# The products of exp(k) with v: two head pairs behind each other in two slots, in place of four slots

## The chip, the core and the metric

One NeuronCore of a Trainium2 chip runs the whole program. The metric is device time in microseconds, the median of several executions. The profile shows one further execution, recorded instruction by instruction. Engines are named as the profile names them: PE (TensorE, matmuls), PEld (its weight loads), DVE (VectorE), ACT (ScalarE), POOL (GpSimd), SP (SyncE, which issues the loads and stores).

## The reference

Linear attention over 8 batches of 8 heads with 576 tokens and 64 channels, followed by a two-layer network on the 4608 tokens, all in float32:

```python
q_s = softmax over channels of q;  k_s = softmax over tokens of k
kv  = einsum('bhsd,bhse->bhde', k_s, v)      # 64 x 64 per head
att = einsum('bhsd,bhde->bhse', q_s, kv)     # tokens x 512 when heads are joined
h   = att @ w_in                             # 512 -> 2048
g   = max(h, 0) + log1p(exp(-abs(h)))
out = g @ w_out                              # 2048 -> 512
```

## The kernel before, in words

**Tiles and slots.** The 4608 tokens are cut into 9 tiles of 512. Tile t is one *stage* of the program (stage 0 to 8). The network's 2048 inner channels are cut into 16 blocks of 128; block j of tile t is one *slot* (slot 0 to 15 of stage t). In a slot TensorE first does `up(t, j)`: 12 matmuls of 128x512, a value split into a high and a low float32r part, three products for each of four head pairs, into one of two PSUM tiles `ph`. Then, two slots late, it does `down` for an earlier block: 12 matmuls into four PSUM tiles `po`. In stage 0 the split is not used, and there are eight float32 matmuls in a slot.

**Softplus.** Between `up` and `down`, ScalarE runs Abs, Exp, Copy and Ln (L384 to L387) and casts the result (`g_hi`, L395); VectorE runs three combined operations (L388 to L390) and the difference `g_lo` (L396). The cast and `g_lo` of a slot stand in the program of the next slot.

**Attention, spread over the slots.** While stage t runs, `attend(t + 1)` puts the attention of the next tile into its slots. A list `steps` of 17 entries names which step stands in which slot; `lazy` registers a unit's steps and their slots. For batch t + 1 there are four units `kv_unit`, one for each pair of heads, with six steps:

- `top`: maximum of k over tokens on VectorE (L182); the maximum over partitions follows, by a TensorE transpose in batches 1 and 2 (`ON_PE`), from batch 3 on by GpSimd (L187);
- `across`: only in batches 1 and 2: a second maximum and transpose (L198, L199);
- `shift`: subtraction of the maximum on VectorE (L203);
- `product`: Exp on ScalarE (L209); the matmuls of exp(k) with v (L214, ten in the program, each 64 columns wide, alternating between the upper and lower half of one of two PSUM tiles, `banks`, named att in the profile) are put behind the slot's `down`. Behind them `kv_prefetch` loads a later pair into the buffer that they free (`kp` has two buffers);
- `scale`: 1/sum, on VectorE (L224, L225);
- `split`: `kv_hi` on ScalarE (L238) and `kv_lo` on VectorE (L241).

The softmax of q (`q_unit`, 12 steps, L265 to L304) stands in slots 3 to 10. In slots 11 to 14, `x_unit` joins both, one head pair in each slot: a transpose on VectorE (L321) into the same PSUM tile, a cast on ScalarE (`q_hi`, L325), a difference on VectorE (`q_lo`, L326), and the matmuls L331 to L333 at the slot's end; the results are split in the next slot (L339, L340), those of the last two pairs behind slot 15.

In stages 0 and 1 there is also the preparation of weights (L115 to L146); the last of it, a split of 1.2 us on VectorE in each slot (L145, L146), runs through slot 14 of stage 1.

**Order.** All of this is written out by hand under `manual_schedule`: each engine runs its instructions in the order in which the program issues them. Within a slot it is `up`, the attention's steps (units in the order of registration: kv, then q, then x), `split_g` of the slot before, `softplus`, `down`, and last the matmuls kept back by `later`.

Of the kernel before, what the change touches and what calls it, by code (L numbers as in the profile page):

```python
# [54 lines left out]
def tile_attn_ffn(  # L55
# [38 lines left out]
    def load_w(k):  # L94
        raw[k] = wp.tile([P, 2, DM], I64, name=f"w{k}")
        nc.sync.dma_start(out=raw[k][:, 0], in_=w_in[k])
        nc.sync.dma_start(out=raw[k][:, 1], in_=w_out[k])
# [24 lines left out]
    def sign_w(k, engine=nc.vector):  # L122

        if engine is nc.vector:
            high, low = (raw[k].bitcast(U8).rearrange("p z (n e) -> p (z n) e", e=8)[:, :, e] for e in (7, 3))
            engine.tensor_scalar(out=low, in0=high, scalar1=0x80, scalar2=None, op0=ALU.bitwise_and)  # L126
        else:
            engine.tensor_scalar(
                out=halves(k, BF16)[1], in0=words(k, F32)[1], scalar1=2.0**-100, scalar2=2.0**-100,
                op0=ALU.mult, op1=ALU.mult,  # L130
            )
# [123 lines left out]
    def q_load(t):  # L255
        qt = qp.tile([P, HP * TOK], F32, name="qt")
        nc.sync.dma_start(out=qt, in_=q[:, HP * START[t]:HP * START[t + 1]])
        qtiles[t] = qt.rearrange("p (h n) -> p h n", h=HP)
# [58 lines left out]
    def x_unit(t, h, ps):  # L317


        def flip():  # L320
            nc.vector.transpose(ps, qtiles[t][:, h])  # L321

        def product():
            q_hi, q_lo = (qp.tile([P, TOK], F32R, name=name) for name in ("q_hi", "q_lo"))
            nc.scalar.copy(q_hi, ps)  # L325
            nc.vector.tensor_tensor(out=q_lo, in0=ps, in1=q_hi.bitcast(F32), op=ALU.subtract)  # L326

            def products():
                for b, c0, c1 in segments(t):
                    hi, lo = kv_hi[b % 2][h], kv_lo[b % 2][h]  # L330
                    nc.tensor.matmul(ps[:, c0:c1], lhsT=hi, rhs=q_hi[:, c0:c1], start=True, stop=False)  # L331
                    nc.tensor.matmul(ps[:, c0:c1], lhsT=lo, rhs=q_hi[:, c0:c1], start=False, stop=False)
                    nc.tensor.matmul(ps[:, c0:c1], lhsT=hi, rhs=q_lo[:, c0:c1], start=False, stop=True)  # L333

            later(products)

        def split():
            x = x_part(t, h)
            nc.scalar.copy(x[:, 0], ps)  # L339
            nc.vector.tensor_tensor(out=x[:, 1], in0=ps, in1=x[:, 0].bitcast(F32), op=ALU.subtract)  # L340

        return [flip, product, split]

    def x_first(h, bank):


        def flip():
            nc.vector.transpose(qT[:, h], qtiles[0][:, h])

        def product():  # L350
            nc.tensor.matmul(bank, lhsT=whole[:, h], rhs=qT[:, h], start=True, stop=True)

        def take():
            if h % 2 == 0:
                nc.scalar.copy(x0[:, h], bank)
            else:
                nc.vector.tensor_copy(x0[:, h], bank)

        return [flip, product, take]
# [75 lines left out]
    def kv_prefetch(**place):  # L435
        if ahead[0] < len(kv_order):
            bh = kv_order[ahead[0]]
            loaded[bh] = kv_load(*bh, **place)
            ahead[0] += 1

    with tc.manual_schedule():

        make_identity(nc, ident)
        q_load(0)
        for i in range(HP):
            place = dict(pool=xp, tag=f"x{i - 1}", shape=(P, HP * TOK)) if i >= 2 else {}
            kv_prefetch(engine=nc.vector, queue=nc.scalar, **place)
        for k in range(5):
            load_w(k)
        nc.vector.memset(zero, 0.0)  # L450

        nc.scalar.activation(ln1, zero, AF.Ln, bias=1.0)
        whole = wp.tile([P, HP, P], F32, name="spare")
        qT = wp.tile([P, HP, TOK], F32, name=f"w{NJ - 1}")
        x0 = xp.tile([P, HP, TOK], F32, name="x0")
        for z in [whole] + [z.bitcast(F32) for i in range(2) for z in kv_hi[i] + kv_lo[i]]:
            nc.vector.memset(z, 0.0)

        po = [ps_o.tile([P, DM], F32, name=f"po{h}") for h in range(HP)]
        units = [kv_unit(0, h, po[h]) for h in range(HP)]
        first = [x_first(h, po[h]) for h in range(HP)]
        todo = {f"q{i}": fn for i, fn in enumerate(q_unit(0))}
        for h in range(HP):
            todo.update({f"u{h}{i}": fn for i, fn in enumerate(units[h])})
            todo.update({f"x{h}{i}": fn for i, fn in enumerate(first[h])})
        for k in range(2):
            for name, fn in (("t", top_w), ("m", scale_w), ("s", lambda k: sign_w(k, nc.gpsimd)), ("j", join_w)):
                todo[f"{name}{k}"] = lambda k=k, fn=fn: fn(k)  # L470
        todo["kv"] = kv_prefetch
        todo["w"] = lambda: [load_w(k) for k in range(5, 10)]
        todo["q"] = lambda: [q_load(1)] + [load_w(k) for k in range(10, NJ)]
        for name in (
            "q0 q1 u00 q2 q3 q4 q5 u10 u01 u11 u02 u12 q6 u03 u13 u20 u30 u21 u31 u22 u32 u23 u33 t0 m0 s0 q7 q8 "
            "kv kv w u04 u14 u05 u15 q9 q10 q11 x00 x10 x01 x11 u24 u34 u25 u35 x20 x30 x02 x12 t1 m1 s1 x21 x31 j0 "
            "x22 x32 q"
        ).split():
            todo[name]()

        def attend(t):

            steps = [[] for _ in range(NJ + 1)]

            def lazy(make, slots):
                unit = []

                def step(i):
                    def fn():
                        if not i:  # L490
                            unit.extend(make())
                        unit[i]()
                    return fn

                for i, s in enumerate(slots):
                    steps[s].append(step(i))

            if t < B:
                on_pe = 1 if t <= ON_PE else 0
                for h in range(HP):  # L500
                    a = 2 * h
                    lazy(
                        lambda h=h: kv_unit(t, h, banks[h % 2], after=kv_prefetch),
                        [a, a + on_pe, a + 1 + on_pe, a + 2 + on_pe, a + 3 + on_pe, a + 3 + on_pe],
                    )
            lazy(lambda: q_unit(t), [3, 4, 5, 5, 6, 7, 8, 7, 8, 9, 9, 10])
            for h, slots in enumerate(([11, 11, 12], [12, 12, 13], [13, 13, NJ], [14, 14, NJ])):
                lazy(lambda h=h: x_unit(t, h, banks[h % 2]), slots)
            if t + 1 < NTILE:
                steps[14].append(lambda: q_load(t + 1))  # L510
            return steps

        order = [(t, j) for t in range(NTILE) for j in range(NJ)]
        pending, soft, waiting = [], None, []
        for n in range(len(order) + 3):
            slot = order[n] if n < len(order) else None
            if slot:
                t, j = slot
                if j == 0:
                    steps = attend(t + 1) if t + 1 < NTILE else [[] for _ in range(NJ + 1)]  # L520
                ph = up(t, j)
                for fn in steps[j]:
                    fn()
                if t == 0 and 1 <= j <= HP:
                    split_whole(j - 1)
                if t == 0 and j + 1 < NJ:
                    join_w(j + 1)
                for k in range(NJ):
                    if n == 10 + 4 * k // 3:
                        split_w(k)  # L530
                if j == NJ - 1:
                    for fn in steps[NJ]:
                        fn()
            if soft:
                pending.append((soft[0], split_g(soft[1]) if soft[0][0] else soft[1]))
                soft = None
            if slot:
                soft = slot, softplus(t, j, ph)
                if t == 0 and j + 2 < NJ:
                    for fn in (top_w, scale_w, sign_w):  # L540
                        fn(j + 2)
            while pending and order.index(pending[0][0]) <= n - 2:
                (t, j), g = pending.pop(0)
                down(t, j, g)
            for products in waiting:
                products()
            waiting.clear()
# [37 lines left out]
```

## Time and profile before

| | us |
|---|---|
| median of 3 runs (lowest, highest) | 929.53 (928.31, 929.96) |
| profiled execution | 928.47 |
| its span | 926.6 |
| PE busy | 886.7 (96%) |
| DVE busy | 703.8 (76%) |
| ACT busy | 581.7 (63%) |

The span runs from the first to the last instruction recorded; the execution's own time is 1.9 us longer. The mean granted clock of TensorE is 0.993 of full speed. A busy share is an average over stages with different limits. Stages begin at 34.55 (0), 160.63 (1), 267.24 (2), 361.69 (3), 456.02 (4), 550.83 (5), 645.43 (6), 740.25 (7) and 830.03 (8), by the first `up` matmul of each in the timeline of PE.

### The profile page before, as it was taken

How to read it: one execution, taken by the hardware profiler on the slowest of the kernel's cores; microseconds unless marked ns; L12 is line 12 of the kernel's file. 1: busy time of each engine (PE TensorE's matmuls, PEld its weight loads, DVE VectorE, ACT ScalarE, POOL GpSimd, SP SyncE). 2: the span in 40 equal slices, each digit the busy share in tenths (PEclk: the TensorE clock that was granted, in tenths of full speed). 3: DMA queues.
4: the chain of work that ended last, by engine and by line, in shares of the span. 5: the costliest groups of instructions: out<-in, count | busy, mean ns of one | idle time of the engine just before them, and what ended most of it. 6: DMA issues, size and time to landing. Idle time of an engine off the chain costs nothing.

```text
span 926.6 us, 11575 instructions
## 1 busy us (share of the span) xinstructions
PE 886.7 (96%) x4180; PEld 675.3 (73%) x4180; DVE 703.8 (76%) x1095; ACT 581.7 (63%) x982; POOL 56.4 (6%) x118
## 2 busy tenths in 40 slices
PE   2698999999899999999999999999999999999998
PEld 2243444677688888888888888888888888888886
DVE  8679888788878877787778778877787757765553
ACT  3666676756666656666567566656665666566554
POOL 1302200000001100110011000100110000000000
PEclk9899999999999999999999999999999999999999
DMA  9970101111013101210121012101200110001001
GB/s 315 381 298 26 35 17 46 45 53 52 1 46 97 52 1 46 89 43 18 46 71 52 27 46 71 52 26 46 71 27 1 46 46 1 1 1 46 0 1 46
DMA packets 49034, 55.28 MB, mean 60 GB/s; under 512 B 2256, under 2 KB 39120, under 8 KB 47824
## 3 DMA queue, kind: packets, MB, share of 16 engines
q1 hardware_dynamic: 48400, 54.27, 17.4%
q8 instruction: 33, 0.54, 0.2%
q10 hardware_dynamic: 576, 0.26, 0.1%
q14 instruction: 25, 0.20, 0.1%
HBM read 45.09 MB, written 9.44 MB: 59 GB/s over the span
## 4 chain that ended last, share of the span: by engine, by line
PE 76%; DVE 12%; ACT 8%; issue 3%; DMA 1%; POOL 0%; SPq 0%; DVEq 0%; ACTq 0%; POOLq 0%
PE ph L372 11%; PE ph L374 11%; PE ph L373 11%; PE po L418 11%; PE po L416 11%; PE po L417 11%; PE ph L367 3%; PE po L412 3%; PE att L214 2%; DVE w L126 1%; DVE l L390 1%; DVE w L389 1%; DVE w L388 1%; PE att L331 1%; ACT u L385 1%
## 5 line engine op out<-in xcount | busy, mean ns | idle before, releaser
L372 PE MATMUL ph<-x,w 128*128 128x512 f32 x480 | 191.7, 399 | 0.0
L418 PE MATMUL po<-w,g_lo 128*128 128x512 f32 x480 | 187.0, 390 | 1.4 <-DVE g_lo L396 1.4
L374 PE MATMUL ph<-x,w 128*128 128x512 f32 x480 | 188.0, 392 | 0.0
L373 PE MATMUL ph<-x,w 128*128 128x512 f32 x480 | 187.6, 391 | 0.0
L416 PE MATMUL po<-w,g_hi 128*128 128x512 f32 x480 | 186.8, 389 | 0.0
L417 PE MATMUL po<-w,g_hi 128*128 128x512 f32 x480 | 186.7, 389 | 0.0
L388 DVE SCALAR_TENSOR_TENSOR w<-w,u 128x512 f32<-128x512 f32 x128 | 88.4, 691 | 108.8 <-ACT w L386 108.8
L395 ACT CAST g_hi<-l 128x512 fp32r<-128x512 f32 x128 | 79.7, 622 | 92.3 <-DVE l L390 89.8
L390 DVE SCALAR_TENSOR_TENSOR l<-l,ln,w 128x512 f32<-128x512 f32 x128 | 96.3, 752 | 15.7 <-DVE w L389 1.4
L418 PEld LDWEIGHTS po<-w,g_lo 128*128 128x128 f32 x480 | 90.1, 188 | 21.2 <-DVE g_lo L396 2.6
L372 PEld LDWEIGHTS ph<-x,w 128*128 128x128 f32 x480 | 90.8, 189 | 19.3 <-issue 0.6
L374 PEld LDWEIGHTS ph<-x,w 128*128 128x128 f32 x480 | 90.4, 188 | 19.7
L417 PEld LDWEIGHTS po<-w,g_hi 128*128 128x128 f32 x480 | 90.1, 188 | 18.7
L416 PEld LDWEIGHTS po<-w,g_hi 128*128 128x128 f32 x480 | 90.1, 188 | 18.6
L373 PEld LDWEIGHTS ph<-x,w 128*128 128x128 f32 x480 | 90.7, 189 | 17.6 <-DVE w L146 0.2
L384 ACT ACTIVATE u<-ph 128x512 f32<-128x512 f32 x134 | 80.1, 598 | 33.5 <-PE ph L374 25.0
L396 DVE TENSOR_TENSOR g_lo<-l,g_hi 128x512 fp32r<-128x512 f32 x128 | 88.4, 691 | 15.5 <-ACT g_hi L395 15.3
L387 ACT ACTIVATE l<-u 128x512 f32<-128x512 f32 x128 | 79.3, 619 | 25.8 <-DVE g_lo L396 25.2
L389 DVE SCALAR_TENSOR_TENSOR w<-ph,w 128x512 f32<-128x512 f32 x128 | 88.5, 691 | 4.4
L385 ACT ACTIVATE u<-u 128x512 f32<-128x512 f32 x134 | 84.7, 632 | 4.3
L386 ACT ACTIVATE w<-u 128x512 f32<-128x512 f32 x128 | 80.9, 632 | 4.1
L325 ACT CAST q_hi<-att 128x512 fp32r<-128x512 f32 x32 | 18.8, 587 | 78.6 <-DVE att L321 78.6
(125 smaller groups left out, 1061.1 us busy)
## 6 DMA issues: line engine op xcount, KB each, us to landing
kvt<-in_kv SPq DMA_DIRECT2D x30, 512.0 KB, 4.2
qt<-in_q SPq DMA_DIRECT2D x9, 1024.0 KB, 4.9
w<-in_w_in SPq DMA_DIRECT2D x16, 512.0 KB, 10.2
w<-in_w_out SPq DMA_DIRECT2D x16, 512.0 KB, 10.2
out<-w SPq DMA_DIRECT2D x32, 256.0 KB, 2.3
kvt<-in_kv_tail SPq DMA_DIRECT2D x28, 64.0 KB, 3.9
x<-in_kv SPq DMA_DIRECT2D x2, 512.0 KB, 9.4
out<-x SPq DMA_DIRECT2D x4, 256.0 KB, 2.4
```

Of the source, the lines that this page charges most:

```text
L372: nc.tensor.matmul(ph, lhsT=w_hi, rhs=x_hi, start=h == 0, stop=False)
L373: nc.tensor.matmul(ph, lhsT=w_lo, rhs=x_hi, start=False, stop=False)
L374: nc.tensor.matmul(ph, lhsT=w_hi, rhs=x_lo, start=False, stop=h == HP - 1)
L385: nc.scalar.activation(u, u, AF.Exp, scale=-1.0)
L386: nc.scalar.activation(w, u, AF.Copy, bias=1.0)
L388: nc.vector.scalar_tensor_tensor(out=w, in0=w, scalar=1.0, in1=u, op0=ALU.subtract, op1=ALU.subtract)
L389: nc.vector.scalar_tensor_tensor(out=w, in0=ph, scalar=0.0, in1=w, op0=ALU.max, op1=ALU.subtract)
L390: nc.vector.scalar_tensor_tensor(out=l, in0=l, scalar=ln1, in1=w, op0=ALU.subtract, op1=ALU.add)
L396: nc.vector.tensor_tensor(out=g_lo, in0=l, in1=g_hi.bitcast(F32), op=ALU.subtract)
L416: nc.tensor.matmul(po, lhsT=g_hi[:, ms], rhs=w_hi, start=j == 0, stop=False)
L417: nc.tensor.matmul(po, lhsT=g_hi[:, ms], rhs=w_lo, start=False, stop=False)
L418: nc.tensor.matmul(po, lhsT=g_lo[:, ms], rhs=w_hi, start=False, stop=j == NJ - 1)
```

## The change

Only the slots of the steps of `kv_unit` are different, and only for t > 1, so in `attend(2)` to `attend(7)`, which run in stages 1 to 6. The first and second pair form a couple, and the third and fourth. Within a couple `top` and `shift` stand one slot apart, and `product`, `scale` and `split` stand in the same slots. No instruction is added or removed.

```diff
--- before.py
+++ after.py
@@ -499,9 +499,15 @@
                 on_pe = 1 if t <= ON_PE else 0
                 for h in range(HP):
                     a = 2 * h
+                    slots = [a, a + on_pe, a + 1 + on_pe, a + 2 + on_pe, a + 3 + on_pe, a + 3 + on_pe]
+                    if t > 1:
+
+                        a = (5 + on_pe) * (h // 2)
+                        c = a + h % 2 + on_pe
+                        slots = [c - on_pe, c, c + 1] + [a + on_pe + i for i in (3, 4, 4)]
                     lazy(
                         lambda h=h: kv_unit(t, h, banks[h % 2], after=kv_prefetch),
-                        [a, a + on_pe, a + 1 + on_pe, a + 2 + on_pe, a + 3 + on_pe, a + 3 + on_pe],
+                        slots,
                     )
             lazy(lambda: q_unit(t), [3, 4, 5, 5, 6, 7, 8, 7, 8, 9, 9, 10])
             for h, slots in enumerate(([11, 11, 12], [12, 12, 13], [13, 13, NJ], [14, 14, NJ])):
```

The slots that this gives (top, across, shift, product, scale, split; `across` does nothing from batch 3 on):

| pair | stage 1 before | stage 1 after | stages 2 to 6 before | stages 2 to 6 after |
|---|---|---|---|---|
| 0 | 0 1 2 3 4 4 | 0 1 2 4 5 5 | 0 0 1 2 3 3 | 0 0 1 3 4 4 |
| 1 | 2 3 4 5 6 6 | 1 2 3 4 5 5 | 2 2 3 4 5 5 | 1 1 2 3 4 4 |
| 2 | 4 5 6 7 8 8 | 6 7 8 10 11 11 | 4 4 5 6 7 7 | 5 5 6 8 9 9 |
| 3 | 6 7 8 9 10 10 | 7 8 9 10 11 11 | 6 6 7 8 9 9 | 6 6 7 8 9 9 |

On TensorE, at the end of a slot in stage 3, the program before has one pair's matmuls between the last `down` matmuls (po3) and the next slot's `up` (ph). This is slot 2:

```order
L417 MATMUL po3_2767<-spare_755,g_hi_2697 128x512
L418 MATMUL po3_2767<-spare_755,g_lo_2698 128x512
L214 MATMUL att0_105<-kvt_2182 64x65 x10
L372 MATMUL ph_2796<-x2_2452,w2_901 128x512
L373 MATMUL ph_2796<-x2_2452,w2_901 128x512
L374 MATMUL ph_2796<-x2_2452,w2_901 128x512
```

After the change, slot 2 has none, and at the end of slot 3 there are two, into both att tiles:

```order
L418 MATMUL po3_2767<-w0_786,g_lo_2751 128x512
L214 MATMUL att0_105<-kvt_2266 64x65 x10
L214 MATMUL att1_106<-kvt_2282 64x65 x10
L372 MATMUL ph_2856<-x2_2452,w3_929 128x512
L373 MATMUL ph_2856<-x2_2452,w3_929 128x512
L374 MATMUL ph_2856<-x2_2452,w3_929 128x512
```

So the matmuls of the second pair moved from the end of slot 4 to the end of slot 3, behind those of the first, which moved there from slot 2.

On VectorE, at the beginning of slot 9 of stage 3, between the last operation of softplus (L390) and that of the next slot, the program before has one pair's `scale` and `split` (L224 to L241, att1), then the last steps of q (L265 to L304), then `g_lo` (L396):

```order
L390 SCALAR_TENSOR_TENSOR l_3093<-l_3093,ln1_109,w_3092 128x512
L224 TENSOR_SCALAR r_3142<-att1_106 128x1
L225 RECIPROCAL r_3142<-r_3142 128x1
L241 SCALAR_TENSOR_TENSOR kv_lo03_100<-att1_106,r_3142,kv_hi03_92 64x64 x2
L265 COPY other_3149<-s_2818 32x64 x4
L300 SCALAR_TENSOR_TENSOR s_2818<-s_2818,other_3149 128x64
L301 RECIPROCAL s_2818<-s_2818 128x64
L304 TENSOR_TENSOR qt_2562<-qt_2562,s_2818 128x1024
L396 TENSOR_TENSOR g_lo_3158<-l_3093,g_hi_3157 128x512
```

After the change it has two pairs' in the same place:

```order
L390 SCALAR_TENSOR_TENSOR l_3070<-l_3070,ln1_109,w_3069 128x512
L224 TENSOR_SCALAR r_3135<-att0_105 128x1
L225 RECIPROCAL r_3135<-r_3135 128x1
L241 SCALAR_TENSOR_TENSOR kv_lo02_99<-att0_105,r_3135,kv_hi02_91 64x64 x2
L224 TENSOR_SCALAR r_3142<-att1_106 128x1
L225 RECIPROCAL r_3142<-r_3142 128x1
L241 SCALAR_TENSOR_TENSOR kv_lo03_100<-att1_106,r_3142,kv_hi03_92 64x64 x2
L265 COPY other_3149<-s_2796 32x64 x4
L300 SCALAR_TENSOR_TENSOR s_2796<-s_2796,other_3149 128x64
L301 RECIPROCAL s_2796<-s_2796 128x64
L304 TENSOR_TENSOR qt_2562<-qt_2562,s_2796 128x1024
L396 TENSOR_TENSOR g_lo_3158<-l_3070,g_hi_3157 128x512
```

The group that reads att0 moved here from slot 7; what follows it is in the same order as before.

## Rows read from the trace of the kernel before

**Rows 1.** The page: busy time, share of the span and instructions of each engine.
```profile
PE 886.7 (96%) x4180; PEld 675.3 (73%) x4180; DVE 703.8 (76%) x1095; ACT 581.7 (63%) x982; POOL 56.4 (6%) x118
```

**Rows 2.** Busy time by stage, stages 1 and 3 (columns: window, length, engines, clock, DMA).
```profile
160.63:267.24 106.61, 100.82 (x491) 77.63 (x490) 86.38 (x132) 70.55 (x116) 1.88 (x12) 0.98 0.13 43
...
361.69:456.02 94.33, 94.23 (x489) 77.06 (x488) 74.55 (x120) 60.21 (x107) 6.36 (x16) 1.00 0.15 48
```

**Rows 3.** Timeline of TensorE, stage 5, slots 2 and 3 (start, length, instruction).
```profile
566.70 0.39 PE L417 MATMUL po<-spare,g_hi 128*128 128x512 f32 x1
566.92 0.39 PE L418 MATMUL po<-spare,g_lo 128*128 128x512 f32 x1
567.24 0.80 PE L214 MATMUL att<-kvt 128*64 128x65 f32 x20
567.97 0.50 PE L372 MATMUL ph<-x,w 128*128 128x512 f32 x1
568.31 0.40 PE L373 MATMUL ph<-x,w 128*128 128x512 f32 x1
```

**Rows 4.** Groups of VectorE by line (busy, mean of one, idle before).
```profile
L182 DVE TENSOR_REDUCE mx<-kvt 128x128 f32<-128x640 f32 x30 | 39.8, 1328 | 1.8 <-DMA kvt<-in_kv_tail 1.3 <-DMA kvt<-in_kv 0.4
...
L296 DVE TENSOR_REDUCE s<-qt 128x32 f32<-128x1024 f32 x18 | 21.7, 1212 | 0.0
...
L203 DVE TENSOR_TENSOR kvt<-kvt,mx 128x640 f32<-128x640 f32 x20 | 16.5, 826 | 0.4
```

**Rows 5.** Timeline of ScalarE, stage 3, slot 8.
```profile
409.60 0.74 ACT L209 ACTIVATE kvt<-kvt 128x640 f32<-128x640 f32 x1
410.24 1.04 ACT L293 ACTIVATE qt<-qt 128x1024 f32<-128x1024 f32 x1
411.58 0.62 ACT L395 CAST g_hi<-l 128x512 fp32r<-128x512 f32 x1 [0.30 <-DVE l L390]
412.11 0.59 ACT L384 ACTIVATE u<-ph 128x512 f32<-128x512 f32 x1
```

**Rows 6.** Timeline of VectorE, stage 3, slot 9 and the start of 10.
```profile
416.25 0.15 DVE L224 TENSOR_SCALAR r<-att 128x1 f32<-128x1 f32 x1
...
417.96 0.78 DVE L265 COPY other<-s 32x64 f32<-32x64 f32 x4
...
419.04 0.55 DVE L301 RECIPROCAL s<-s 128x64 f32<-128x64 f32 x1
...
420.77 0.68 DVE L396 TENSOR_TENSOR g_lo<-l,g_hi 128x512 fp32r<-128x512 f32 x1
...
422.89 0.75 DVE L390 SCALAR_TENSOR_TENSOR l<-l,ln,w 128x512 f32<-128x512 f32 x1
423.56 1.22 DVE L304 TENSOR_TENSOR qt<-qt,s 128x1024 f32<-128x1024 f32 x1
```

**Rows 7.** Timeline of VectorE and TensorE, slot 13 of stages 3 and 6.
```profile
442.82 0.69 DVE L326 TENSOR_TENSOR q_lo<-att,q_hi 128x512 fp32r<-128x512 f32 x1 [0.65 <-ACT q_hi L325]
...
443.57 0.39 PE L331 MATMUL att<-q_hi,kv_hi 128*128 128x256 f32 x1
...
726.33 0.69 DVE L326 TENSOR_TENSOR q_lo<-att,q_hi 128x512 fp32r<-128x512 f32 x1 [0.65 <-ACT q_hi L325]
...
727.43 0.36 PE L331 MATMUL att<-q_hi,kv_hi 128*128 128x448 f32 x1
```

**Rows 8.** Waits of weight loads, stages 2 to 6 (total, times, longest).
```profile
PEld att L331 <- DVE q_lo L326: 2.9, 8, 0.5
```

**Rows 9.** Timeline of VectorE and TensorE, stage 1, slots 1, 4 and 11.
```profile
172.49 0.69 DVE L388 SCALAR_TENSOR_TENSOR w<-w,u 128x512 f32<-128x512 f32 x1 [2.75 <-ACT w L386]
...
190.62 1.32 DVE L182 TENSOR_REDUCE mx<-kvt 128x128 f32<-128x640 f32 x1 [1.33 <-DMA kvt<-in_kv_tail]
...
239.31 0.33 PE L331 MATMUL att<-q_hi,kv_hi 128*128 128x128 f32 x1 [1.76 <-DVE q_lo L326]
```

**Rows 10.** The page: DMA issues (times, KB each, us to landing).
```profile
kvt<-in_kv SPq DMA_DIRECT2D x30, 512.0 KB, 4.2
```

## The prediction, on record before the changed kernel ran

> **What bounds the kernel now.** I read the page first: TensorE is busy for 96% of the span [rows 1], so at first sight only TensorE's time counts. A table by stage (a stage is the 16 slots of one token tile) says the same for most of the run: stage 3 has 94.23 us of TensorE in 94.33, and stage 1 has only 100.82 in 106.61 [rows 2]. The timeline of TensorE gives its rates. Matmuls of 128x512 start every 0.227 us, so a slot of 24 costs 5.44 us. The products of one head pair (20 short matmuls in the trace) take 0.73 us, and around them two steps are longer than 0.227: 0.32 into them and 0.34 out of them [rows 3].
>
> "Busy" hides a second bound. In slots 11 to 14 TensorE needs, at the end of the slot, the `q_lo` that VectorE makes in that slot. In slot 13 of stage 3, `q_lo` ends at 442.82 + 0.69 = 443.51 and TensorE's L331 starts at 443.57, right behind it; in stage 6 the same instruction starts 0.41 behind, so it has 0.35 to spare [rows 7]. Waiting for `q_lo` costs weight loads 2.9 us in 8 places of stages 2 to 6 [rows 8]; they lie in stages 2 to 5. So the end of a stage hangs on how late VectorE is when it enters slot 11. That is what I work out; the TensorE saving alone is not the answer.
>
> **What the change removes.** In stages 1 to 6 there are four clusters of products per stage before and two after, so 12 joins. Each saves one step in and one step out: 0.32 - 0.227 + 0.34 - 0.227 = 0.2 us, 2.5 us over the run, as far as TensorE sets the time. The trace has no seam of two pairs. It is bounded by 0 (the seam is as dear as leaving and entering) and 0.25 (nothing, and the slightly slow matmuls behind a cluster vanish too). I take 0.2.
>
> The Trainium skill (TensorEngine Tiling (Array Packing), Key Properties) says that a change of tiling mode drains the engine, not a change of tile within a mode. Rows 3 agree as far as they go: both long steps stand where 128x64 meets 128x128. By that rule alone the change would be worth the 2.5 us; it is the first rival below.
>
> **What it moves, stages 2 to 6.** The order shows it: in slot 9 VectorE now has two `r`/`kv_lo` groups where it had one, ahead of the inverse, the division and `g_lo`. Starts on VectorE in rows 6 give: one group 417.96 - 416.25 = 1.71 (with its wait for ScalarE's `kv_hi`), inverse and division 420.77 - 417.96 = 2.81, the FFN's four 423.56 - 420.77 = 2.79. Each instruction starts about 0.08 before the one ahead ends (422.89 + 0.75 against 423.56).
>
> Does VectorE start slot 9 early enough to make up for 1.71? Walk it from the stage's start, in us. TensorE's slots now start: slot 4 at 3 x 5.44 + 5.44 + 0.09 + 2 x 0.73 = 23.3, then 28.9, 34.4, 39.8, slot 8 at 45.2, slot 9 at 52.2, slot 11 at 63.2 (63.7 before). The soonest VectorE can be through a slot's chain is 7.1 after the slot's start: `up` ends 11 x 0.227 + 0.39 = 2.9 into it, ScalarE starts L384 about 0.1 behind that, and from L384 to VectorE's next work 416.25 - 412.11 = 4.14 pass [rows 5, 6].
> - Slot 3 leaves it free at 16.3 + 7.1 = 23.4.
> - Slot 4: two groups 3.42, one pass over q 1.13, 2.79; with 0.4 for L384, which stands behind the second `kv_hi`: 31.2.
> - Slot 5: maximum of k 1.25, the swap and join 1.1 (as 419.04 - 417.96), a pass 1.14, 2.79: 37.5.
> - Slot 6: subtraction of k 0.74, maximum 1.25, pass 1.14, 2.79: 43.4. (Durations of one less 0.08 [rows 4].)
> - Slot 7: 0.74 + 1.13 + 2.79 and 0.2 for ScalarE: 48.3.
> - Slot 8: little VectorE work, but ScalarE now does two Exps of k and one of q (0.64 + 0.64 + 0.95, rows 5) before L395 and L384. L387 can start at 46.1, when slot 7's `g_lo` has read its tile; with 0.5 for it, 2.23 and 0.5 for L395, L384 starts at 49.3, and VectorE is free at 49.3 + 4.14 = 53.5.
>
> Before, that point was 416.25 - 361.69 = 54.6. So VectorE starts slot 9 1.0 earlier and has 1.7 more to do: it is 0.7 later from there through slot 11. No idle time takes it back before slot 13, since there each instruction follows the other through ScalarE (L326 is preceded by 0.65 of waiting for `q_hi`, rows 7). So in stages 2 to 5, where L331 in slot 13 already follows `q_lo`, the stage ends 0.7 later, and the 0.4 that TensorE saved in it is lost in the wait. In stage 6 it is 0.7 - 0.35 = 0.35. Together 4 x 0.7 + 0.35 = 3.1 us.
>
> Bounds: if slot 8 were caught up, VectorE would be free at 45.2 + 7.1 = 52.3, and `q_lo` 0.6 earlier than before; the stage then gains TensorE's 0.4. If the backlog of slots 5 and 6 is 0.6 larger, `q_lo` comes 1.3 later. So -2 to +6.2 for the five stages; I take +3.1, the walk.
>
> **Stage 1** is limited by VectorE, which also prepares weights there: TensorE waits 1.76 us for `q_lo` at 239.31 [rows 9]. VectorE's total work does not change, but its idle time does. The maximum of the third pair waits 1.33 us for its load [rows 9], because the products that free the buffer stand only one slot ahead of it (3 and 4); now they stand two ahead (4 and 6), and a load lands in 4.2 us [rows 10]. And VectorE waits 2.75 us before 172.49 in slot 1 [rows 9], into which the second pair's maximum moves, 1.25; of that most comes out of later slots, but I count only 0.3, because slots 2 and 3 get idle time in exchange. So -1.3 - 0.3 = -1.6. Bounds: nothing, if the waits reappear as ScalarE's; -2.6, if the whole 1.25 counts.
>
> **At no cost:** two k/v loads now go out together behind slot 3 or 8. Their users stand in slots 5 and 6, where VectorE reads them at 31.2 at the earliest, 7.9 after the products end; SyncE has no output to store there. If that cover went, it would be a wait like the 1.33 per stage. GpSimd's reductions keep one slot between maximum and subtraction. The second Exp of a joined pair is done long before TensorE reaches the cluster at the slot's end.
>
> **Sum.** 3.1 - 1.6 = +1.5 us. The profiled execution took 928.47 us (span 926.6, 1.9 around it); with the change 930.0. It lies 1.06 under the median of the runs, 929.53, on which I put the same difference: **931.0 us**.
>
> **Rivals.**
> *TensorE decides (faster).* VectorE's delay is covered, joins pay everywhere: 2.5 us saved, and 1.3 for the load in stage 1: -3.8, 925.7 us. For it: TensorE is 96% busy [rows 1], and stage 6 has room in slot 13 [rows 7]. Against: the other four stages have none. The rule on tiling modes cited above speaks for this one. It decides if VectorE starts slot 9 at least 1.7 earlier than before.
> *The double split blocks VectorE for longer (slower).* In slot 9, and in slot 11 of stage 1, the second group waits for ScalarE's `kv_hi` behind the first. If VectorE enters slot 9 no more than 0.5 earlier than now, `q_lo` is 1.2 late in each stage: 4 x 1.2 + 0.85 = 5.6, less 1 in stage 1: +4.6, 934.1 us. For it: slots 5 and 6 carry 6.3 and 5.9 us of VectorE against 5.44 of TensorE. Against: slots 7 and 8 give the backlog back in my walk.
> *It does nothing new on TensorE:* the seam costs what two switches do. Since VectorE sets the ends, that changes the forecast by 0.5 at most and is part of it.
>
> **Chances.** Forecast 0.50 (its own range -0.5 to +3, 929.0 to 932.5), TensorE decides 0.21, longer block 0.29. About 0.2%, 1.86 us, is what a measurement tells from no change. The forecast, at +1.5, splits 0.36 within and 0.14 slower; the first rival 0.19 faster and 0.02 within; the second 0.26 slower and 0.03 within. So faster 0.19, within 0.41, slower 0.40. The range, 925.6 to 934.4, holds the forecast and most of both rivals.
>
> **What would show it.** Clusters of 40 matmuls in slots 3 and 8 (stage 1: 4 and 10), with no long step inside. Slot 9 of stages 2 to 6 begins on VectorE about 53.5 after the stage's start and `q_lo` of slot 11 ends about 69.5 (68.8 before). TensorE waits for `q_lo` in slots 11, 12 and 13, and stages 2 to 5 last about 0.7 longer each. Stage 1 is about 1.6 shorter, without the wait for `kv_tail`. The forecast is wrong if stages 2 to 5 get shorter, or if TensorE waits for something else than `q_lo`.

## The result, and the profile after

| | before | after |
|---|---|---|
| median of 6 runs (lowest, highest), us | 929.71 (928.31, 929.98) | 932.54 (931.60, 933.52) |
| profiled execution, its span | 928.47, 926.6 | 931.60, 929.8 |
| stage 1 | 106.61 | 104.65 (-1.96) |
| stages 2, 3, 4, 5, 6 (after: the difference) | 94.45, 94.33, 94.81, 94.60, 94.82 | +1.19, +1.29, +0.67, +0.96, +0.95 |
| stages 0, 7 and 8 together, to the end of the last matmul | 308.73 | +0.06 |

The ratio over all runs is 1.0035, 95% interval [1.0023, 1.0046] (the two medians alone give 1.0030): slower, by more than the 0.2% that a measurement of this kernel can tell. The 3.2 us between the two spans are +5.06 in stages 2 to 6, -1.96 in stage 1 and +0.06 elsewhere.

The chain that ended last (followed back from the last instruction, at each step to what released it), on the page before:

```profile
PE 76%; DVE 12%; ACT 8%; issue 3%; DMA 1%; POOL 0%; SPq 0%; DVEq 0%; ACTq 0%; POOLq 0%
```

The page after: busy times, and the same chain.

```profile
PE 885.6 (95%) x4180; PEld 674.9 (73%) x4180; DVE 704.5 (76%) x1095; ACT 580.6 (62%) x982; POOL 55.1 (6%) x118
...
PE 52%; DVE 26%; ACT 15%; issue 6%; DMA 1%; POOL 0%; DVEq 0%; ACTq 0%; POOLq 0%
```

TensorE is still busy for 95% (96% in [rows 1]), but its share of the chain fell from 76% to 52%, and that of VectorE and ScalarE together rose from 20% to 41%. Busy time by stage, stages 1 and 3 after, with the columns of [rows 2]:

```profile
160.69:265.34 104.65, 100.00 (x491) 77.98 (x490) 86.07 (x132) 70.19 (x116) 1.88 (x12) 0.98 0.14 43
360.98:456.60 95.62, 94.16 (x489) 76.94 (x488) 74.79 (x120) 60.01 (x107) 6.17 (x16) 1.00 0.15 48
```

In stage 3 TensorE was without work for 0.10 us [rows 2]; now it is for 95.62 - 94.16 = 1.46. The weight loads' waits ahead of the clusters of products (L214) in stages 2 to 6, before, then the waits of TensorE and its weight loads there, after (total, times, longest):

```profile
PEld att L214 <- issue: 7.0, 20, 0.4
```

```profile
PEld att L331 <- DVE q_lo L326: 11.2, 15, 1.4
PE att L331 <- DVE q_lo L326: 5.1, 5, 1.0
PEld att L214 <- issue: 3.5, 10, 0.4
PEld po L418 <- DVE g_lo L396: 2.5, 5, 0.7
PE po L418 <- DVE g_lo L396: 0.5, 2, 0.3
```

The weight loads' 2.9 us in 8 places [rows 8] have become 11.2 in 15: slots 11, 12 and 13 of all five stages. The wait for `g_lo` is new, once per stage, in slot 10. The 0.35 us at each cluster is still paid, but 10 times in place of 20: that part of the joins' saving is there, though the stages are longer. TensorE at the joined cluster of stage 3, slot 8, after:

```profile
411.26 0.39 PE L418 MATMUL po<-w,g_lo 128*128 128x512 f32 x1
411.57 1.39 PE L214 MATMUL att<-kvt 128*64 128x65 f32 x40
412.89 0.50 PE L372 MATMUL ph<-x,w 128*128 128x512 f32 x1
413.23 0.40 PE L373 MATMUL ph<-x,w 128*128 128x512 f32 x1
```

Forty matmuls take 412.89 - 411.57 = 1.32 us, where twice the twenty of [rows 3] would be 1.46; the steps into and out of the cluster are 0.31 and 0.34 as before, once instead of twice. VectorE in slot 11 of stage 3, before, and then in slots 9 to 11 of stage 3, after, answering [rows 6]:

```profile
429.79 0.69 DVE L326 TENSOR_TENSOR q_lo<-att,q_hi 128x512 fp32r<-128x512 f32 x1 [0.65 <-ACT q_hi L325]
```

```profile
414.81 0.15 DVE L224 TENSOR_SCALAR r<-att 128x1 f32<-128x1 f32 x1
...
415.92 0.58 DVE L241 SCALAR_TENSOR_TENSOR kv_lo<-att,r,kv_hi 64x64 fp32r<-64x64 f32 x2 [0.76 <-ACT kv_hi L238]
416.53 0.16 DVE L224 TENSOR_SCALAR r<-att 128x1 f32<-128x1 f32 x1
...
417.94 0.58 DVE L241 SCALAR_TENSOR_TENSOR kv_lo<-att,r,kv_hi 64x64 fp32r<-64x64 f32 x2 [1.05 <-ACT kv_hi L238]
418.53 0.79 DVE L265 COPY other<-s 32x64 f32<-32x64 f32 x4
...
421.34 0.68 DVE L396 TENSOR_TENSOR g_lo<-l,g_hi 128x512 fp32r<-128x512 f32 x1
...
430.36 0.69 DVE L326 TENSOR_TENSOR q_lo<-att,q_hi 128x512 fp32r<-128x512 f32 x1 [0.65 <-ACT q_hi L325]
```

VectorE starts slot 9 at 414.81 - 360.98 = 53.83 after the stage's start (54.6 before) and has the block of two groups, 3.72 us up to L265 (3.43 to 3.44 in the other four stages, where the second `kv_hi` is not late). So `g_lo` is late for slot 10's `down`, and `q_lo` of slot 11 ends at 430.36 + 0.69 - 360.98 = 70.07 (before, 429.79 + 0.69 - 361.69 = 68.79). TensorE after, in slots 10 and 11:

```profile
422.08 0.50 PE L418 MATMUL po<-w,g_lo 128*128 128x512 f32 x1 [0.28 <-DVE g_lo L396]
...
429.70 0.39 PE L418 MATMUL po<-w,g_lo 128*128 128x512 f32 x1
431.11 0.39 PE L331 MATMUL att<-q_hi,kv_hi 128*128 128x256 f32 x1 [1.02 <-DVE q_lo L326]
```

Stage 1, after: `kv_tail` is no longer waited for, nor, but for 0.3 us of a weight load, is the maximum, and one long wait for `q_lo` is left at slot 11, 3.46 us where it was 1.76 [rows 9]. What the maximum L182 waited for in stage 1, and who waited for it, before:

```profile
  DMA kvt<-in_kv_tail: 1.3, 1
...
  PEld att L184: 2.9, 2
  PE att L184: 2.1, 2
```

and TensorE at slot 11 of stage 1, after:

```profile
237.26 0.33 PE L331 MATMUL att<-q_hi,kv_hi 128*128 128x128 f32 x1 [3.46 <-DVE q_lo L326]
```

### The profile page after: what moved, and what is told of

It reads as the page before. It is cut to its first block, busy times and chain, and to the rows that moved or that the text cites. A ratio compares the mean times of both kernels' runs of the same rounds, so it can differ in the third digit from the quotient of the medians.

```text
span 929.8 us, 11610 instructions
## 1 busy us (share of the span) xinstructions
PE 885.6 (95%) x4180; PEld 674.9 (73%) x4180; DVE 704.5 (76%) x1095; ACT 580.6 (62%) x982; POOL 55.1 (6%) x118
## 4 chain that ended last, share of the span: by engine, by line
PE 52%; DVE 26%; ACT 15%; issue 6%; DMA 1%; POOL 0%; DVEq 0%; ACTq 0%; POOLq 0%
PE ph L372 7%; PE ph L373 7%; PE ph L374 7%; PE po L418 7%; PE po L417 7%; PE po L416 7%; DVE w L389 3%; DVE w L388 3%; PE ph L367 3%; DVE l L390 3%; PE po L412 3%; ACT u L385 2%; ACT w L386 2%; ACT u L384 2%; DVE mx L182 2%
## 5 line engine op out<-in xcount | busy, mean ns | idle before, releaser
L388 DVE SCALAR_TENSOR_TENSOR w<-w,u 128x512 f32<-128x512 f32 x128 | 88.5, 691 | 110.8 <-ACT w L386 110.1
L390 DVE SCALAR_TENSOR_TENSOR l<-l,ln,w 128x512 f32<-128x512 f32 x128 | 96.3, 752 | 15.0 <-DVE w L389 0.5
L384 ACT ACTIVATE u<-ph 128x512 f32<-128x512 f32 x134 | 80.1, 598 | 31.4 <-PE ph L374 23.3
L396 DVE TENSOR_TENSOR g_lo<-l,g_hi 128x512 fp32r<-128x512 f32 x128 | 88.5, 691 | 14.8 <-ACT g_hi L395 14.8
```

Of the source, the lines that this page charges most:

```text
L384: nc.scalar.activation(u, ph, AF.Abs)
L388: nc.vector.scalar_tensor_tensor(out=w, in0=w, scalar=1.0, in1=u, op0=ALU.subtract, op1=ALU.subtract)
L390: nc.vector.scalar_tensor_tensor(out=l, in0=l, scalar=ln1, in1=w, op0=ALU.subtract, op1=ALU.add)
```

## The experiments

The theory: TensorE saves time at each join, but in stages 2 to 6 the block of two groups in slot 9 makes VectorE late at slot 11, and the stage ends as late as `q_lo`. Rivals: the seam of two clusters costs TensorE as much as it saves, or the doubled work of ScalarE in slots 3 and 8 is what delays. Ratios are to the kernel before, from runs on the same chip. Stage columns are differences in us to the kernel before, from the profiled executions; the wait is that of weight loads for `q_lo` in stages 2 to 6 (2.9 us in 8 places in the kernel before).

| run | median us | ratio [95%] | stage 1 | stages 2 to 6, sum | wait for `q_lo` |
|---|---|---|---|---|---|
| e1 | 926.05 | 0.9969 [0.9958, 0.9981] | -2.01 | +0.08 | 3.0, 9 places |
| e2 | 933.37 | 1.0046 [1.0034, 1.0059] | 0.00 | +4.79 | 11.1, 15 |
| e7 | 927.60 | 0.9991 [0.9981, 1.0001] | -2.01 | +0.44 | 8.6, 15 |
| e6 | 930.00 | 1.0012 [1.0003, 1.0021] | -2.02 | +2.84 | 10.5, 15 |
| e3 | 935.15 | 1.0065 [1.0051, 1.0080] | -2.01 | +8.34 | 11.4, 15 |
| e5 | 927.32 | 0.9982 [0.9973, 0.9991] | +0.04 | -1.66 | none |
| e4 | 924.13 | 0.9944 [0.9930, 0.9958] | -2.00 | -3.02 | 4.5, 12 |
| e8 | 923.39 | 0.9945 [0.9933, 0.9958] | -1.97 | -3.85 | 3.2, 8 |
| e10 | 921.10 | 0.9915 [0.9902, 0.9929] | -1.98 | -5.81 | none |
| e11 | 922.28 | 0.9928 [0.9916, 0.9941] | -2.01 | -5.04 | 1.4, 4 |
| e9 | 924.93 | 0.9954 [0.9940, 0.9967] | -0.76 | -3.45 | 4.1, 11 |

Stage 0, whose program is the same everywhere, was 1.0 to 1.1 us longer in the profiled executions of e3, e4, e5, e6, e8 and e11, at a granted clock of 0.97 in that stage against 0.99 before and after, and 0.5 shorter in that of e9; so mechanisms are read from stages 1 to 6 and not from the totals.

**e1 and e2: each part of the change alone.** Edits to the changed kernel:

```diff
-                    if t > 1:
+                    if t == 2:   # e1: new slots in stage 1 only
+                    if t > 2:    # e2: new slots in stages 2 to 6 only
```

> The change in batch 2 alone (stage 1); batches 3 to 7 as before. Theory (VectorE sets the end of each stage, and the change makes it late in stages 2 to 6 but takes a wait for a load out of stage 1): stage 1 is 1.9 us shorter, the other stages as before, so -1.9 us, ratio 0.998. Rival (the joined cluster costs something wherever it stands, 3.2 us over 6 stages): stage 1 is 0.5 longer, ratio 1.0005.

> The change in batches 3 to 7 alone (stages 2 to 6); batch 2 as before. Theory: stages 2 to 6 are 0.7 to 1.3 us longer each, +5.1 us, ratio 1.0055, and TensorE's wait for q_lo in slot 11 stands in all five. Rival (the joined cluster costs the same in each stage): +2.7 us, ratio 1.003.

Both came out by the theory: -2.0 us in stage 1, +4.8 in stages 2 to 6, and these add up to the change (-1.96, +5.06) within 0.3 us. The two ratios multiply to 1.0015 only, less than the change's 1.0035; the intervals are 0.0023 to 0.0025 wide. The change is two changes of opposite sign.

**e7: the last pair's `scale` and `split` leave slot 9.** The join on TensorE stays; VectorE gets one group in slot 9 and one in slot 10.

```diff
+                        if t > 2 and h == 3:
+                            slots[4:] = [10, 10]
```

> The change, but in batches 3 to 7 scale and split of the fourth pair stand in slot 10 in place of 9. Theory: VectorE has as much to do before slot 11, but in slot 10 it waits 0.83 us for ScalarE before L388, and the group takes the place of most of that; q_lo of slot 11 is 0.6 to 0.7 earlier than with the change, TensorE's wait for g_lo in slot 10 is gone; stages 2 to 6 about 0.6 shorter than with the change, ratio to the kernel before 1.0003. Rival (two groups in one slot): all of the loss of stages 2 to 6 is gone, ratio 0.998.

The wait for `g_lo` is gone and the stages are 4.6 us shorter than after the change, 0.92 each where 0.6 was expected, so the result lies between theory and rival: taking one group out of slot 9 gives back most of what the stages had lost, but not the joins' saving. `q_lo` of slot 11 ends at 428.23 + 0.69 - 360.12 = 68.80 in stage 3, as in the kernel before, and that stage is as long as before (94.31 against 94.33), though it has two joins. Waits for `q_lo` in slots 11 to 13 remain.

**e6: no two Exps in one slot.** The Exp of the first and third pair stands one slot earlier. (The lines that split `product` into `power`, the Exp, and the rest are left out here.)

```diff
-        return [top, across, shift, product, scale, split if b else keep]
+        return [top, across, shift, product, scale, split if b else keep, power]
...
+                        if t > 2 and h % 2 == 0:
+                            slots.append(a + 2)
```

> The change, but in batches 3 to 7 the Exp of the first and third pair stands one slot ahead of its matmuls, so that ScalarE has one Exp of k in slots 3 and 8 and not two. Theory: in slot 8, L395 then waits for VectorE's L390 and not for ScalarE, 0.3 earlier; q_lo is 0.3 earlier and each of stages 2 to 6 is 0.3 shorter than with the change: ratio to the kernel before 1.0018. Rival (the two Exps in a row are what makes VectorE late): the stages get back 1.0 each, ratio 0.998.

The stages are 2.2 us shorter than after the change, 0.44 each on average, where 0.3 was expected and the rival had 1.0: ScalarE's doubled work in slots 3 and 8 is a part of the loss, and less than half of it.

**e3: the second couple apart.** Stages 2 to 6 keep one join, at slot 3; the third pair's matmuls stand in slot 7 and its group in slot 8, one slot ahead of the fourth's.

```diff
+                        if t > 2 and h == 2:
+                            slots = [5, 5, 6, 7, 8, 8]
```

> The change, but in batches 3 to 7 the products of the third pair stand in slot 7 and its scale and split in slot 8, so that slot 9 has one group on VectorE again. Theory (what counts is when VectorE is through with all that stands before slot 11): the group now stands in slot 8, in front of ScalarE's Exps and L384, which are what VectorE waits for there; slot 9 begins about 2 us later and has 1.7 to 2.0 less to do, so q_lo is as late as with the change, and stages 2 to 6 are still 1.0 to 1.3 longer each: ratio 1.0035. Rival (two groups in one slot are what blocks VectorE): stages 2 to 6 lose nothing, ratio 0.998.

The rival is out, and the theory's size was missed too: 3.3 us longer than after the change, though slot 9 has one group. ScalarE at L384 of slot 8 of stage 3, after the change, and then ScalarE in slot 8 of stage 3, e3:

```profile
410.66 0.59 ACT L384 ACTIVATE u<-ph 128x512 f32<-128x512 f32 x1
```

```profile
411.09 0.63 ACT L238 ACTIVATE kv_hi<-att,r 64x64 fp32r<-64x64 f32 x2 [2.08 <-DVE r L225]
411.75 0.75 ACT L209 ACTIVATE kvt<-kvt 128x640 f32<-128x640 f32 x1
412.40 1.04 ACT L293 ACTIVATE qt<-qt 128x1024 f32<-128x1024 f32 x1
413.35 0.60 ACT L395 CAST g_hi<-l 128x512 fp32r<-128x512 f32 x1
413.97 0.60 ACT L384 ACTIVATE u<-ph 128x512 f32<-128x512 f32 x1
```

`kv_hi` waits 2.08 us for VectorE's `r`, and an Exp of k, q's Exp and all of slot 8's softplus stand behind it. L384 starts at 413.97 - 361.98 = 51.99 after the stage's start, against 410.66 - 360.98 = 49.68 after the change, and VectorE enters slot 9 at 418.14 - 361.98 = 56.16 against 53.83: 2.3 later, with one group of 1.7 less to do. `q_lo` of slot 11 ends 0.3 to 0.8 later than after the change (70.38 to 70.58 against 69.75 to 70.07). So "two groups in one slot" alone is not the cause: what counts is how late VectorE is when it enters slot 11, and what stands behind it on ScalarE on the way there.

**e5 and e4: q's steps one slot earlier, without and with the change.** VectorE works ahead where it has room, in slots 2 to 4.

```diff
-            lazy(lambda: q_unit(t), [3, 4, 5, 5, 6, 7, 8, 7, 8, 9, 9, 10])
+            e = 1 if t > 2 else 0
+            lazy(lambda: q_unit(t), [s - e for s in (3, 4, 5, 5, 6, 7, 8, 7, 8, 9, 9, 10)])
```

> The kernel before, with the steps of q's softmax one slot earlier in batches 3 to 7; the products in four slots. Theory: it only takes away the waits for q_lo that the kernel before had in slot 13, 0.1 to 0.25 us in four stages: -0.7 us, ratio 0.9993. Rival (q's place in itself is worth what e4 gains): as much as e4 in stages 2 to 6, -4.5 us, ratio 0.995.

> The change, with the steps of q's softmax one slot earlier in batches 3 to 7, so that VectorE has 1.1 us less to do in slot 10 and 1.7 less in slot 9. Theory: q_lo of slot 11 is ready before TensorE's down matmuls end, the waits in slots 10 and 11 are gone, and the two joins of a stage then pay their 0.8 us: stages 2 to 6 are 0.8 to 1.0 shorter than before the change, stage 1 1.9 shorter: -6.5 us, ratio 0.993. Rival (the joined cluster itself costs): stages 2 to 6 no shorter than before, ratio 0.998 or more.

e5 gained more than expected (1.66 for 0.7) and no wait for `q_lo` is left in it: its mean stage, 94.60 - 0.33 = 94.27 us, is what TensorE needs with four clusters (it is busy for all of the 93.80 us of stage 3). The rival had as much as e4: e5 has 1.66 of e4's 3.02 us. e4 turned the loss into a gain, but with less than expected (-3.0 for -4 to -5): weight loads still wait in 12 places.

**e8: q's steps two slots earlier, with the change** (`e = 2` in the same edit).

> The change, with the steps of q's softmax two slots earlier in batches 3 to 7. Theory: VectorE enters slot 11 with nothing left over, q_lo has over 1 us to spare there and the period of 6.52 us in slots 12 and 13 no longer reaches TensorE; a stage gains the 0.8 of its two joins and the 0.1 to 0.25 that it waited before: stages 2 to 6 are 0.9 to 1.1 shorter than before the change, stage 1 2.0 shorter: -7 us, ratio 0.9925. Rival (what is left of the wait comes from the joined clusters and not from q's place): as with q one slot earlier, ratio 0.9944 to 0.996.

A miss: -3.85 for -4.5 to -5.5, and the ratio is that of e4, as the rival had it. VectorE ends slot 10's softplus (L390) 8.85 us after that slot's start in stage 3; 7.2 is the soonest that a slot shows in any of these kernels, 10.61 the changed kernel's. The block in slot 9 is still there, so this run alone does not tell whether it or the joined clusters keep the rest; e10 does.

**e10: both reliefs** (the edits of e8 and e7 together).

> The change with both reliefs of slot 9, for t > 2 (stages 2 to 6): q's twelve steps two slots earlier, and the fourth pair's scale and split in slot 10. The theory (TensorE's joins pay about 0.4 us each, and only VectorE's lateness at slot 11 takes them away): VectorE enters slot 11 with little backlog, waits for q_lo all but vanish (below 2 us over five stages), and stages 2 to 6 become about 0.8 us shorter each than before the change in full, with the two joins; with the two us of stage 1 the run takes about 6 us less than before, ratio 0.993 to 0.994. The rival (the joins pay only the 0.2 of the forecast, and the rest of the gain seen with q earlier was q's): stages 2 to 6 about 0.4 shorter than before, as in the kernel before with q one slot earlier plus nothing, ratio 0.9955 or more.

Now TensorE and its weight loads wait for neither `q_lo` nor `g_lo` in stages 2 to 6. All that the view of waits has left of them there, e10:

```profile
PEld att L214 <- issue: 3.5, 10, 0.4
```

and the chain that ended last, e10's page:

```profile
PE 80%; DVE 10%; ACT 6%; issue 3%; DMA 1%; POOL 0%; DVEq 0%; ACTq 0%; POOLq 0%
```

VectorE in slots 9 to 11 of stage 3, e10:

```profile
412.30 0.15 DVE L224 TENSOR_SCALAR r<-att 128x1 f32<-128x1 f32 x1
...
413.41 0.58 DVE L241 SCALAR_TENSOR_TENSOR kv_lo<-att,r,kv_hi 64x64 fp32r<-64x64 f32 x2 [0.76 <-ACT kv_hi L238]
414.06 0.69 DVE L396 TENSOR_TENSOR g_lo<-l,g_hi 128x512 fp32r<-128x512 f32 x1
416.01 0.69 DVE L388 SCALAR_TENSOR_TENSOR w<-w,u 128x512 f32<-128x512 f32 x1 [1.26 <-ACT w L386]
...
425.43 0.69 DVE L326 TENSOR_TENSOR q_lo<-att,q_hi 128x512 fp32r<-128x512 f32 x1 [0.65 <-ACT q_hi L325]
```

VectorE has 1.26 us of waiting to spare before L388, where the changed kernel ran without a gap, and its `q_lo` of slot 11 ends 67.26 after the stage's start. TensorE is busy for all of the 92.97 us of stage 3. The mean stage is 93.44 us, against e5's 94.27 with four clusters and no wait for `q_lo`: the two joins are worth 0.83 per stage (0.82 to 0.84 in each of the five), 0.41 each. Against the kernel before a stage is 1.16 shorter, these 0.83 and the 0.33 of e5; the theory had 0.8, the rival 0.4. e10 is 0.8% faster than the kernel before; of the other runs' intervals only e11's overlaps its own.

**e11: e10 with the Exp of e6.**

> The same as the kernel ahead of it (q two slots earlier, fourth pair in slot 10), and in addition the Exp of the first and third pair one slot earlier, so that ScalarE no longer does two Exps of k in slots 3 and 8; all for t > 2. The theory: slot 8 no longer holds VectorE back, so it enters slot 9 about 0.4 earlier; where the kernel ahead still waits for q_lo, these waits go, at most 0.2 per stage; where it doesn't, no difference: ratio 0.992 to 0.994. The rival (ScalarE's earlier Exp only moves the block one slot ahead): no difference from the kernel ahead of it within 0.1%.

The ratio is the expected one, but the theory missed: waits for `q_lo` came back in four places, in stages 2 and 3 (-0.65 and -1.10 against e10's -1.14 and -1.36); stages 4 to 6 are equal within 0.02. VectorE in slot 2 of stage 3, at the first step of softplus, e10 and then e11 (whose lines are numbered 5 higher):

```profile
374.76 0.69 DVE L388 SCALAR_TENSOR_TENSOR w<-w,u 128x512 f32<-128x512 f32 x1 [0.32 <-ACT w L386]
```

```profile
376.47 0.69 DVE L393 SCALAR_TENSOR_TENSOR w<-w,u 128x512 f32<-128x512 f32 x1 [0.96 <-ACT w L391]
```

With q two slots earlier, slot 2 is no longer empty: the Exp put there stands ahead of ScalarE's softplus, VectorE waits 0.64 us longer for it, and it enters slot 9 0.4 later than in e10 (53.88 against 53.44 after the stage's start), not 0.4 earlier. In all five stages `q_lo` is later by 0.4 to 0.6. In slot 13 of e10, `q_lo` has 0.27 and 0.38 us to spare ahead of L331 in stages 2 and 3 and 0.58 to 0.90 in stages 4 to 6, so only the first two wait. The intervals of the two ratios overlap.

**e9: e8 with q earlier in stage 1 too** (`e = 2 if t > 1`).

> The change with q's steps two slots earlier for t > 1, so in stage 1 as well as in stages 2 to 6. Stages 2 to 6 as in the run with q two slots earlier for t > 2 (about 0.8 us shorter each than before the change). Stage 1 is the question. If VectorE's lateness there is the sum of its work up to slot 11 with idle time in the first slots left to fill, q earlier fills some of it: stage 1 0.5 to 1.5 us shorter than after the change (2.5 to 3.5 shorter than before). The rival: no idle time is left in the first slots of stage 1, and it is as long as after the change (2.0 shorter than before).

Both expectations missed: stage 1 became 1.2 us longer than after the change. Waits in stage 1, e9:

```profile
PE att L331 <- DVE q_lo L326: 2.9, 2, 2.3
...
PE po L418 <- DVE g_lo L396: 1.1, 1, 1.1
PE att L184 <- DVE mx L182: 1.1, 2, 0.6
...
PE att L199 <- DVE m L198: 0.5, 1, 0.5
```

The wait for `q_lo` shrank from 4.1 to 2.9, but in batch 2 the maxima of k go through TensorE, and with q ahead of them on VectorE they are late again, as in the kernel before. VectorE did have idle time in the first slots: its wait before L388 in slot 1 fell from 2.15 us after the change to 1.03. It got such a wait back later, 1.13 before L388 in slot 9, after TensorE had waited for the maxima and 1.14 for `g_lo` in slot 8, and `q_lo` of slot 11 ends 1.2 later than after the change (77.72 against 76.51).

## Why the prediction was right

The time, 932.54, lies in the stated range, at the upper edge of the forecast's own (929.0 to 932.5) and midway between the forecast, 931.0, and the second rival, 934.1. Slower by over 0.2%, which happened, had a chance of 0.40, just under that of no change, 0.41. The sign and the mechanism were right; the loss in stages 2 to 6 and the gain in stage 1 were both put too small, and these two errors partly cancel in the sum.

- *VectorE sets the ends of stages 2 to 6*: right, and shown by e4, e8 and e10, which leave TensorE's work as the change made it and only relieve VectorE. From stage 2 to 5 the change's `q_lo` of slot 11 is 1.19, 1.28, 0.65 and 0.95 later than before, and the stages 1.19, 1.29, 0.67 and 0.96 longer.
- *0.7 later in each stage*: mis-sized. The mean over the five stages is 1.05. (By the walk's own numbers, 54.6 - 53.5 is 1.1 and not 1.0, and the delay 0.6.) The walk gave 23.4, 31.2, 37.5, 43.4, 48.3 and 53.5 for VectorE's release after slots 3 to 8; stage 3 has 23.47, 31.10, 37.73, 43.83, 48.69 and 53.83. Slots 5 and 6 took 0.3 and 0.2 more than they were costed at, slot 4 0.2 less, and nothing behind them gives it back. So VectorE entered slot 9 only 0.54 to 0.77 earlier than before in the five stages, not 1.0. The second group was costed at 1.71, the length of a single one, and that is what it took in four of the stages; in stage 3 it is 418.53 - 416.53 = 2.00, since `kv_hi` comes late there.
- *Stage 6, with 0.35 to spare*: `q_lo` 1.20 later, the stage 0.95 longer, so 0.25 of the delay was covered. Together +5.06 for the forecast's +3.1.
- *Stage 1, -1.6*: -1.96, and -2.01 in e1. VectorE sets its end: `q_lo` of slot 11 ends at 76.51 after the stage's start, 2.11 earlier than before (78.62). Named were the load's 1.33, which went, and 0.3 for work moved into idle time; VectorE's waits in the stage up to that `q_lo`, added up, fell from 12.8 to 11.1 us, so this term was well sized. The other 0.4 lies in the work between the waits and was not taken apart. TensorE's 2.1 us of waiting for the maxima also went, but as it waits for `q_lo` at slot 11 in any case (1.7 us longer than before), that did not shorten the stage by itself.
- *A join saves 0.2, at most 0.25*: wrong. Two slots with a cluster each and the two behind them last 2 x (6.26 + 5.60) = 23.72 us in stage 3 before; 6.85 + 5.57 and two plain slots of 5.44 are 23.30 after: 0.42, and e10 against e5 gives 0.41. The bound left out that a cluster has a fixed cost inside itself too (1.32 for 2 x 0.73, so 0.14). It did not hurt the sum, but only because the saving is lost in the wait: that is luck. In e10, where the joins pay, they give 0.83 per stage and not 0.4.
- *TensorE waits for nothing but `q_lo`*: not so, and the prediction had named this as a sign of being wrong. It also waits for `g_lo` in slot 10, 0.5 us in two of the five stages (up to 0.28), its weight loads 2.5 in all five. The block in slot 9 is behind this wait as well (in e7 it is gone), so the mechanism stands, with a second place where it shows.
- *The rivals.* "TensorE decides" is what e10 brings about, with more than its price: -7.8 us in stages 1 to 6, for which the prediction had -3.8. "The double split blocks VectorE for longer" has the better size for stages 2 to 6 (+5.6 forecast, +5.06 measured; the forecast had +3.1) but not for stage 1 (-1, -1.96 measured). Its condition, VectorE entering slot 9 no more than 0.5 earlier than before, was nearly met in stages 2 and 6 (0.54) and not in the others (0.73 to 0.77). The rule of the Trainium skill (TensorEngine Tiling (Array Packing), Key Properties), that a change of tiling mode drains the engine, agrees with e10, where each change saved pays; no run shows that draining is the cause. The page gives no price, and the price here is 0.41 us for leaving and entering once less, of which the steps of [rows 3] show half.

## What to carry to other kernels

Before moving work on an engine that looks idle on average, find the slot in which its result is first waited for, and walk the engine's backlog up to there; a saving on the busy engine counts only if that walk arrives no later than before. Two short blocks on an engine in strict order are not one block spread out. Moving one a slot back (e7) paid, moving it a slot ahead (e3) cost, because a long queue of the other engine stood behind it there: look at both engines' order before choosing the slot, and move ahead of the crowded slots what has its data early, but not into a place that earlier work has just filled (e11). When a change splits into stages with different limits, time each part alone: here one was worth -2 us and the other cost 5, and with VectorE relieved in slots 9 and 10 both gained.

## What was not expected of the hardware

- A cluster of short matmuls between large ones costs about 0.41 us by itself, more than the long steps at its ends (0.2) tell; 0.14 of it is inside the cluster. What is left, some 0.06 by difference, lies in the matmuls behind it. The saving is worked out from slots 2 to 5 of stage 3 and from e10 against e5.
- The same `kv_hi` on ScalarE, for the same `r`, began 0.09 us behind it in one group and 0.38 in the next (stage 3: 415.00 + 0.16 to 415.25, 416.73 + 0.16 to 417.27; with the lengths of the L225 rows, 0.16). This is one of the 28 such pairs from stage 0 on; the other 27 began 0.09 to 0.10 behind. It is the same pair, the second in slot 9 of stage 3, that is 0.37 to 0.39 late in e4, e6, e8 and e9, and no pair of the other runs is late, e2's included. Its cause is open.
- Late VectorE work keeps its lateness: from slot 11 to 13 `q_lo` follows `q_lo` at 6.52 us in the kernel before (68.79, 75.31, 81.82) as after (70.07, 76.59, 83.11), and in e10 (67.26, 73.78, 80.29), where TensorE does not wait and its slots there last 6.15. So it is not TensorE's period but that of the exchange between VectorE and ScalarE, and what `q_lo` has to spare ahead of L331 shrinks by nearly 0.4 from slot to slot (1.09, 0.74 and 0.38 in stage 3 of e10).
